# A new written-out order for a gated linear attention and a two-layer MLP on one core

## The chip, the cores and the metric

The kernel runs on one core of one Trainium2 chip. Time is device time in microseconds (us) of one execution; lower is better. Comparisons are made between executions on the same chip.

## What is computed

A gated linear attention with complex decays, for 4 batches, 8 heads, 768 tokens and 48 dimensions per head, and then a two-layer MLP over its output, 3072 tokens of 384 features with 2048 hidden ones:

```python
mag = np.sqrt(a_re * a_re + a_im * a_im)
scale = np.minimum(mag, 0.999) / (mag + 1e-06)
a_re_n, a_im_n = (a_re * scale, a_im * scale)
for t in range(S):
    ar, ai = (a_re_n[:, :, t, :, None], a_im_n[:, :, t, :, None])
    new_re = ar * S_re - ai * S_im
    new_im = ar * S_im + ai * S_re
    kv = np.einsum('bhd,bhe->bhde', k[:, :, t], v[:, :, t])
    S_re, S_im = (new_re + kv, new_im)
    y[:, :, t] = np.einsum('bhd,bhde->bhe', q[:, :, t], S_re)
...
h = x @ w_in
g = np.maximum(h, 0.0) + alpha * np.minimum(h, 0.0)
return (g @ w_out).astype(np.float32)
```

`x` is `y` with heads and dimensions merged. The two MLP weights come as 64-bit floats.

## The kernel before

The program is a set of tasks, each a Python generator that yields before every step (some instructions on one engine) and issues the step when it is resumed. The order of all steps is written out by hand as a text of 4292 letters, `ORDER`. Each letter stands for one task, and `Plan.run` (lines 96 to 98) resumes that task once per letter. What each engine gets, and in which order, follows from this text alone: every engine runs its own instructions in the order in which the letters issue them, and semaphores hold an instruction until its operands are there. A letter's place in relation to steps of other engines sets no time by itself.

```python
    def run(self, order):
        for c in order:
            next(self.tasks[self.LETTERS.index(c)], None)
...
        plan.run(ORDER)
```

The tasks, by letter (lines 950 to 963):

- A to I: nine gate stages (`gates`, line 223). A covers chunk 0 of batch 0 (128 tokens), B chunks 1 and 2, C chunks 3 to 5, and D to I three chunks each of batches 1 to 3. A stage loads `a_re` and `a_im`, works out magnitudes and running products of the decays on ACT, DVE and POOL, and stores decays (`decs`, line 323) and phases (`phs`, lines 421 and 431) to DRAM. L429 is its last DVE product.
- J, K, L: loads on SP's queue. J (`loads`) fetches for each unit queries and keys (`KQ`), phases (`PP`, L587) and decays (`T`, L594, in two halves). K copies values from DRAM to DRAM in the arrangement that a unit needs, L (`loads_v`) fetches values (`V`, `VL`).
- M, N, O: the pieces of the MLP weights and their conversion to 32 bits (ACT, POOL, DVE).
- P to m: 24 units (`unit`, line 645), one for each chunk of 128 tokens. A unit multiplies queries and keys by phases (L661, L663), then goes through six levels of doubling distance, from 1 to 32: a DVE product with the decays (L717), an ACT copy (L740 or L756), small score products on PE (L678), and masks (L702 on DVE, L699 on ACT). Then it transposes keys on PE (L785), ACT copies them to `T` (L787, L788), and PE makes the state products (L797) and the outputs (L817); DVE updates the state (L826, L829), PE adds its part (L841), ACT copies the result (L855) and two DMAs store it (`ysc`, L860).
- n: loads of the MLP input (`xT`, L873), for 14 groups of one chunk (the first and last two) or two chunks.
- o: the MLP (`all_mlp`, line 926). For each group and each of 16 feature blocks: three 128x128 products (L889, two passes each), ACT's relu (L896), DVE's leaky part (L898); then, for each chunk of the group, an output product (L908, two passes) that accumulates over the 16 blocks, and after the last block an ACT copy (L918) and a store.

The small products of the units use parts of the TensorE array (96x32, 64x64, 64x48, 96x48 weights), the transposes 96x128, the MLP's products 128x128. The buffers that bind are one `PP`, two `T`, one `V` and `VL`, three `KQ`, two tiles in PSUM for scores, two for features, one for an output row.

Of the kernel before, what the change touches and what calls it, by code (L numbers as in the profile page):

```python
# [27 lines left out]


ORDER = (  # L30
    "AAABAAAAAMAAAAAAAAAAAAAAAAAMMMBAAAAMJNAAAAAAAANJNNAAABANANAABBAABAJAKJABAAMAAAABBAAAAAABAOAAOAAKABAA"
# [4 lines left out]
    "MDLJLLCNCRMQDQCORQCQQORMCNKRCRoNODDCDOCNRQRCOQCOCCCCCQKOCMJQOLLoCRQLORCDCLLRKoDRQDLLLCCQNooooCQRRLCR"
    "QQDQCCoDJLLDoCCoCDCMoooRoDQoRCQLLLoRoDRRDCCCoooRoQDDCCRRDoNRRODRNRoooRRDooDnRRoRRoooooDOoLLJoRNOoJDo"
    "oooJDLooooRooLNooNoDRooOJRODROSSooRNoLooooooOooSooENooRSooRSoSJSNoRSERRLRSoSSooooOJLLSJLoooDoSooESJL"
    "LSoSSOoSSoJoLoooooEoLSLDSSDooooSoSSSTSJoSSDoooTSSSooDEToooDSESSSJDoSSooToooSooETJTSJLTLooTTDLoDDDDDE"
    "KSoooJToESSDoDTDoEToLoSKSoSDDoKSTTToooDoDoooJooDKEDSSoooDTTTDoLooTooLooooEooToEEJoEooUoTooUDEoooDooT"  # L40
    "DoDDoLTooJTLLLLLLTDooULooooTETTooTooDToEoDUDDDDDDDDTUoUooTTUoEooUnoUKDUDUKKoooToJJJDJEoETTTTLLLoUoDU"
    "DULEEoELoTUooTLKDoUDoELLoKDoTDDooDoDDDoooDEDTToEooLLoEooDoooUoooooTToTooDUooLDoEoTEoUooDooooUUEoooTo"
    "EoEoUoLUUooUUTEoUEEooULEoooUooUoEUKoJJEooEoooUEUJoJUUUUUoVUEUVJUUVFVVEooEUUUVooooooJoVJVEUUoEVFoEVEE"
    "JooVnVJoJooLVooooooFoWooooWVoVoFFVEEEELLLLLLVLLLooVVWooVooooooEVEEoEooWooWooVVVWoLLWWWEEEEEELEEVVVVV"
    "ooEoVooVLooFVWVEooVVJVJFJVJKVWEFVVWWWEoVJEEEEEVooWFLXLLLEEWEEooWooLoLooooLWEVVWEVEWEKWXEVVVVWLLLLWLo"
    "WFoooEWEEEELEoWoVVooWWEEooooLWEFFWooooooWoEJFoJoWooWWWJEEEEWoWWLoXLoLoEFFooooWoWooooJLLWXXXWFWWWoLXL"
    "ooLoXXWWLoJXWFooWoooXoJooFXoooFXXoXoXooXXJooXoLooFoooFoXXXXLoLYLXXoXLXJoonoXXoXoXooXJXoJJFGFYXFoXoYY"
    "FoFooGGoXXXFFXFKoKFKYFXYFFYFXFFooFFJYoLoooooLYoXoYXXXoJoFooLoFYFJFFGoLLLLoooooXoXXXYYoYoYYoYooYJJFoY"
    "oooooJooZoYYFFYYoZYGYoYoFoLFooooZoLoZooooJoFZZYLZYFoYoFFooJYFFFFFFFFFFFFFFFYoYLLLLoKGZGYYYYYJYZYKJoY"
    "YLLZYYGoLZGoooKoLoZYYKooLFFFGLZLLLGZYYFYZYZoFoFFFFFFFFoFKZZoZFFooFooaoFoFoooaooZGoZFLLLZLLFJZoFZFZJZ"  # L50
    "FZooZoFooZZGFFFoFFoonoooFooooGZoZooZaZFZoJZZoJooGoZZoJooZZaoooaaaGaZZZoZZJZLGJZZoaooLLLGoooooaGaoJoo"
    "oLbooKooJooooLGooabGaGbaoaGaoooGoaaoooooaoGoooLLGLooboobooboaabababaGaooaJoLLaaLoaoaooaaoGJLJGGGGoGo"
    "HGaaaHaaaoGJaaoabGGGGJbGLbGLaaLGHoLaaLooLaobcHGoaoooJJbooJoooGooHGbbooLGoHoobbobobcoooGGHbooGcoooooo"
    "oGGGGGGoHooooobbcbHbccbLLcGLLobHLbLooboGKGboGGGGobooobocbbLGcHcoocGoKbcGGJGGGGbbbHbbbKGbcbJGJccGGGcn"
    "LooJLLLGLGLLLcHLLLLLcHooLcoooGobbbcGcbbGGbbccooobGGooGooodoJJooocoHcGcHHGoocodooooooKGoooccJGGHoGooo"
    "oGooGcooococHGoJoHooGcccGdccoJcGcLGooodHHHLoHLooooJKoooLHddodHoHodododGodoooLLoooIcooodIoocdodHLdodc"
    "HcdLcoHdooccLLHLdIJoHHHcHooHoooocoLoodIdoddoKoodocddddoooeooddooLooodoHHooHooHKHoooLoodHoHodJdHHHHoH"
    "HHIJJdddddJedHoHndddHHdJJLdHeooJooLedodooeddeeoeoLooLHeeeIooHoooooHHHHHHHHHHooHKeoeJJeLoIIeooooofoLo"
    "LeLLLfeLLoooooeefIfooooooooeefeeeooefefoeeoHHHHHeeofIHoooHLLoeHfIooHHHooHeHeeeeIHeeeeeefJeHfoHJIoHeL"
    "oefHoJIoHLoJIffoffeJeIIeeLoofoJoooofHLLooofoogIoooffJfoofffoHofofofLooJLLLogofooJKLIofooHLoHogooongo"  # L60
    "HLLfoLgKHgHgooooooooooooofogogJIfgfffffIgIfffHLJIIoogfIIfILHKoHofHfooLLooooooggLgffgoooooogooooggoIo"
    "ooIHffgILIgogIgIogoLoILIoggooIgoJoLoooLoooILILIIoooogogooghIoLgohoggghhgJogJgggJggooKJgJJggIoIooghhJ"
    "gIIIIohoohgoooohoooooIIIIihIJIoIIIoIJoIooioIoohoJLhhJoooooooooLohLhIihIIIIIhiLoLLLLLLLLLLoonohoooooo"
    "hhoooohiohoihoohIIIIIoooihhhiohoJhJohiIhiioohooooIIIIIIIIIohoohhhhhhioooooooohhohooiohihhIIIooooiihh"
    "IiohhiooooooLoihohiJiiiLJLJLoLLLooooiLLLjLiooIIoiiJjooIojjIIioIIooooooooLojjjLIooooooiooioJoLoijoioo"
    "iiIijJiiijJLoIjiiiiiiiiiioIoooooooIiIoLoooInjLLoojjooooooLjjoooojoooJoojjoooJJooLjjjjjjjkkojooojoooo"
    "oooLkoLokLjoooojookkkkkoLLjooLLoLkookojokojjjjjkoJkkokLLokoooojjkJJJoooLooLoooookjookjkkjkokLjkoojoo"
    "kjojkoLokkooLoooooLooooLoooLoooojJolLLkjlLoookkoLokkkjkJkJkkkkkkoookooJlJoooooooookoLookolkJLklJJoko"
    "loooooloooonJooooJomoloolololoooooooooooooLoooooollllomolomloloooooloooooooooooLommlmLlLLooloooooooo"
    "ooooollolloommmmoLoloollooooooolmloLLLLLLoomlommmmllolllooolmommololmlmmlomlllloommLLLLLLmooLooooooo"  # L70
# [930 lines left out]
```

## Time and profile before

| | |
|---|---|
| runs shown | 836.15, 836.07, 830.36 us (median 836.07) |
| profiled execution | 831.98 us, of which the traced span is 830.2 us |
| mean granted TensorE clock | 0.991 |
| DMA | 58.4% of the 16 engines' span, 130.91 MB |
| L908 output products | 294.4 us of PE, 768 passes, mean 497 ns |
| L889 feature products | 296.3 us of PE, 1344 passes, mean 353 ns |
| L717 decay products | 146.8 us of DVE, 120 (of `KQ` with `T`), mean 1226 ns |
| L898 leaky part | 97.5 us of DVE, 224, mean 436 ns |

PE is TensorE's products, PEld its weight loads, DVE VectorE, ACT ScalarE, POOL GpSimd, SP the engine that issues DMAs. Products are pipelined, so a product's duration is longer than its distance to the next one, and the sum of durations of a group can exceed its busy time. "Idle before" and the waits name the engine and line whose result came last. The slices cut the span into 40 equal parts of 20.8 us; a digit is the busy share in tenths.

### The profile page before, as it was taken

The numbers are of one execution on the slowest core, as the hardware profiler recorded it, in microseconds if no ns is written. First come the engines' busy times: TensorE is split into PE (matmuls) and PEld (weight loads), VectorE is DVE, ScalarE is ACT, GpSimd is POOL, SyncE is SP. The second block draws the span as 40 slices with busy tenths as digits, with TensorE's granted clock in tenths as the row PEclk, the third lists the DMA queues.
The fourth block names the chain that finished last, engine by engine and source line by source line (L and its number), as shares of the span: only waits on it lengthen the run. The fifth ranks groups of instructions, "written<-read, shape, count | busy, mean of one in ns | idle before, by whom it ended". The sixth has DMA issues, their size and how long they took to land.

```text
span 830.2 us, 26838 instructions
## 1 busy us (share of the span) xinstructions
PE 692.1 (83%) x11488; PEld 525.0 (63%) x11488; DVE 650.5 (78%) x1020; ACT 441.5 (53%) x937; POOL 215.3 (26%) x293
## 2 busy tenths in 40 slices
PE   0001515789999999989999999999999999999998
PEld 0001414567777776767777777777777777777776
DVE  5999999999998899889998988999658644552112
ACT  7758879467636655564576456653443333333121
POOL 5231222617715601460155007310520000000000
PEclk9999997899999999999999999999999999999999
DMA  7597985785688489728874695458535544311110
GB/s 204 177 263 185 279 206 172 228 216 145 157 241 201 114 217 251 181 69 223 245 176 103 171 263 135 120 140 245 148 82 134 150 112 112 92 38 38 35 30 10
DMA packets 194174, 130.91 MB, mean 158 GB/s; under 512 B 74120, under 2 KB 185864, under 8 KB 194056
## 3 DMA queue, kind: packets, MB, share of 16 engines
q1 hardware_dynamic: 194056, 129.20, 58.4%
q8 instruction: 90, 1.47, 0.8%
q14 instruction: 28, 0.23, 0.1%
HBM read 100.82 MB, written 35.71 MB: 164 GB/s over the span
## 4 chain that ended last, share of the span: by engine, by line
PE 68%; DVE 14%; ACT 4%; POOL 4%; DMA 4%; issue 3%; SPq 2%; DVEq 0%; ACTq 0%; POOLq 0%
PE ps_o L908 27%; PE ps_h L889 26%; PE ps_lv L678 4%; PE ps_y L817 4%; DVE KQ L717 3%; PE ps_kv L797 3%; PE ps_y L841 2%; PE ps_kt L785 2%; DVE gate L338 2%; DMA T<-decs 1%; POOL gate L338 1%; POOL gate L340 1%; DVE gate L340 1%; DVE gate L298 1%; DVE gate L426 1%
## 5 line engine op out<-in xcount | busy, mean ns | idle before, releaser
L908 PE MATMUL ps_o<-w_out_sb,g_sb 128*128 128x384 f32 x768 | 294.4, 497 | 9.9 <-DVE g_sb L898 9.0
L889 PE MATMUL ps_h<-xT,w_in_sb 128*128 128x256 f32 (+1 forms) x1344 | 296.3, 353 | 1.2 <-issue 1.2
L889 PEld LDWEIGHTS ps_h<-xT,w_in_sb 128*128 128x128 f32 x1344 | 232.8, 191 | 71.3 <-issue 2.0
L896 ACT ACTIVATE g_sb<-ps_h 128x256 f32<-128x256 f32 (+1 forms) x224 | 79.0, 353 | 221.4 <-PE ps_h L889 220.5
L898 DVE SCALAR_TENSOR_TENSOR g_sb<-g_sb,al,ps_h 128x256 f32<-128x256 f32 (+1 forms) x224 | 97.5, 436 | 120.7 <-ACT g_sb L896 120.1
L908 PEld LDWEIGHTS ps_o<-w_out_sb,g_sb 128*128 128x128 f32 x768 | 136.1, 190 | 61.2 <-DVE g_sb L898 11.6
L717 DVE TENSOR_TENSOR KQ<-KQ,T 96x1024 f32<-96x1024 f32 x120 | 146.8, 1226 | 27.5 <-PE ps_lv L678 24.2
L678 PE MATMUL ps_lv<-WQ 96*32 96x32 f32 x2304 | 34.4, 204 | 77.5 <-DVE WQ L661 54.2
L678 PEld LDWEIGHTS ps_lv<-WQ 96*32 96x32 f32 x2304 | 26.4, 116 | 97.1 <-DVE WQ L661 54.2
L515 POOL TENSOR_SCALAR top<-top 128x768 f32<-128x768 f32 x16 | 44.8, 2802 | 82.3 <-ACT top L507 70.6
L740 ACT COPY WQ<-KQ 96x1024 f32<-96x1024 f32 x48 | 50.0, 1041 | 10.9 <-DVE KQ L717 10.8
L338 POOL TENSOR_TENSOR gate<-gate 128x72 f32<-128x72 f32 x42 | 25.9, 616 | 114.6 <-ACT gate L368 101.9
L338 DVE TENSOR_TENSOR gate<-gate 128x576 f32<-128x576 f32 (+5 forms) x84 | 48.0, 572 | 1.8 <-ACT gate L368 0.3
L756 ACT COPY W<-KQ 96x512 f32<-96x512 f32 x48 | 30.8, 641 | 31.2 <-DVE KQ L717 23.5
L699 ACT ACTIVATE A<-ps_lv,columns 128x64 f32<-128x64 f32 x144 | 38.1, 335 | 16.0 <-PE ps_lv L678 15.8
L817 PE MATMUL ps_y<-A,VL 64*48 64x64 f32 x2304 | 42.7, 224 | 3.9 <-issue 3.9
L855 ACT COPY T<-ps_y 48x256 f32<-48x256 f32 x96 | 31.4, 366 | 24.8 <-PE ps_y L841 23.9
L817 PEld LDWEIGHTS ps_y<-A,VL 64*48 64x48 f32 x2304 | 40.2, 126 | 5.6 <-issue 5.3
L426 DVE TENSOR_TENSOR gate<-gate 128x1152 f32<-128x1152 f32 (+2 forms) x36 | 43.1, 1219 | 0.4 <-POOL gate L411 0.3
L678 PE MATMUL ps_lv<-KQ,W 96*32 96x32 f32 x1536 | 24.9, 204 | 18.4 <-ACT W L756 18.2
L702 DVE TENSOR_TENSOR A<-ps_lv,mask 128x256 f32<-128x256 f32 x96 | 37.8, 413 | 0.0
L785 PE MATMUL ps_kt<-ident,KQ 96*128 96x96 f32 x192 | 25.7, 258 | 14.3 <-DVE KQ L717 9.3
(106 smaller groups left out, 916.1 us busy)
## 6 DMA issues: line engine op xcount, KB each, us to landing
T<-decs SPq DMA_DIRECT2D x48, 384.0 KB
PP<-phs SPq DMA_DIRECT2D x24, 387.0 KB
...
```

Source lines behind the costliest of these rows:

```text
L338: on(4 * k).tensor_tensor(out=m, in0=w[:, 1::-1].unsqueeze(2).to_broadcast([P, 2, 2, k]), in1=pairs_of(u), op=ALU.mult)
L426: TT(out=m[:, a], in0=U5[:, 1 + a], in1=turned(off3, o)[:, a].unsqueeze(1).unsqueeze(3).to_broadcast([P, L // 2, nb, 2]), op=ALU.mult)
L515: nc.gpsimd.tensor_scalar(out=top, in0=top, scalar1=F64_SMALL, scalar2=None, op0=ALU.max)
L678: nc.tensor.matmul(t[64 * i + j:64 * i + j + HC // 2, p], lhsT=keys(n, g), rhs=queries(n, g), start=True, stop=True)
L717: nc.vector.tensor_tensor(out=x, in0=x if x0 is None else x0, in1=m, op=ALU.mult)
L740: nc.scalar.copy(z.rearrange("p i n t -> p i (n t)").rearrange("p i (m h) -> p m i h", h=h), bass.AP(tensor=KQ.tensor, offset=KQ.offset + ...
L785: nc.tensor.transpose(t[:, p], KQ[:, 1, 4 * i + p], ident[:D2, :D2])
L817: nc.tensor.matmul(o, lhsT=Vp[h][64 * i:64 * i + 64, s, e_ * D:(e_ + 1) * D], rhs=a, start=False, stop=False)
L889: nc.tensor.matmul(p, lhsT=w_in_sb[:, f // 2, kk, f % 2 * P:(f % 2 + 1) * P], rhs=x_of[m][:, kk], start=(kk == 0), stop=(kk == NK - 1))
L896: nc.scalar.activation(gt, p, AF.Relu, scale=-1.0)
L898: nc.vector.scalar_tensor_tensor(out=gt, in0=gt, scalar=al_1[:, f:f + 1], in1=p, op0=ALU.mult, op1=ALU.add)
L908: nc.tensor.matmul(sums[0], lhsT=gt[:, c * P:(c + 1) * P], rhs=w_out_sb[:, f], start=(f == 0), stop=(f == NF - 1))
```

## The change

Only the text `ORDER` (lines 30 to 77) is replaced. The old and new texts have the same 4292 letters, each letter equally often, in another sequence; tasks, steps, instructions, tiles and buffers are the same. The new text comes from a planner that counts each change from small to large products dearer, and reads packet ends from the finished program; the planner itself is no part of the kernel. The first and last lines that differ:

```diff
 ORDER = (
-    "AAABAAAAAMAAAAAAAAAAAAAAAAAMMMBAAAAMJNAAAAAAAANJNNAAABANANAABBAABAJAKJABAAMAAAABBAAAAAABAOAAOAAKABAA"
-    "LMAAABAAABABBBLBALBABOAOMBAABLBBBNABAABABNAABABBNBABALABLOBOMBNBBKKONOBOBBNBBBJLBOBJBOBLBNBBBJBBBBBB"
-    "NBBNBBBKOBBPBPBPBBBBOPOLBNPBBCJBPCLOMBBCMNBKKBPKKKKBBPPBPMKCBPBBBOKOBCPBBBPPCBLBBJPPLPBNPKCCJCBCPCCC"
...
-    "oooooooooooooooooooooooooooommmmmmmmmmmmmmmoooooooooooooooooooonoooooooooooooooooooooooooooooooooooo"
+    "AAAAAAAAAABAAAAAAAAAAAAAAAMMMMAABAJJMAJJNAAANNLABANAAAABAAAABANAMBAAAABAMAAAANAAALAABKAAOBBAKAKAAAAA"
+    "KBBLLLBAAAALAOBABAAABKKBABOABABAABBMBBBAAKABABALABBBBOANBABABOANBNNBOOBKNOBKBONBNBLNOBBBBBMOBBBOBBJB"
+    "BBBBBKONBKJBPBBBPBBBBOBOOPPBKNJPBNBBCCMPOBBKBBPCCPBKKKMPCBBOBBNBPBPBPBCBBBCBLBPMKNJJPLBPLBBBPPBPPLLC"
...
+    "oLoooooooooooooooooooooooooomooooomommmmmmmmmmommmmmnooooooooooooooooooooooooooooooooooooooooooooooo"
     "oooooooooooooooooooooooooooooooooooooooooooooooooooooooooooooooooooooooooooooooooooooooooooo")
```

More of the change, by code (lines that the diff above doesn't have):

```diff
@@ L30 @@
 ORDER = (
-    "AAABAAAAAMAAAAAAAAAAAAAAAAAMMMBAAAAMJNAAAAAAAANJNNAAABANANAABBAABAJAKJABAAMAAAABBAAAAAABAOAAOAAKABAA"
-    "LMAAABAAABABBBLBALBABOAOMBAABLBBBNABAABABNAABABBNBABALABLOBOMBNBBKKONOBOBBNBBBJLBOBJBOBLBNBBBJBBBBBB"
-    "NBBNBBBKOBBPBPBPBBBBOPOLBNPBBCJBPCLOMBBCMNBKKBPKKKKBBPPBPMKCBPBBBOKOBCPBBBPPCBLBBJPPLPBNPKCCJCBCPCCC"
-    "JNNPCPCPBPCOLCPPPPPPPKNPCKPKNLJCPPJJPCDNPPKCPJCCCNDCPPOJKKCQPCNNPCPPOLJLNOCLCCMOMQCPQQCOQCQQCQCQCDPL"
-    "PDQPPPQCDDQQQCLQPNJCCOCQCOQCQCCQCNDCJLRCQQKQCCLnNJCRJLCDDDQQOCORNCCQNQQLOOQQCLKCOKCKRDCoDJNLDRNQCCNC"
@@ L36 @@
[L36 to L70, printed above, removed]
@@ L71 @@
-    "oomooolollooooooooooooooooooooooooooLooooooommmLLoLonooooooooooomLLmoooooooooooooooooooooooooooooooo"
-    "oooooooooooooooooooooooooooommmmmmmmmmmmmmmoooooooooooooooooooonoooooooooooooooooooooooooooooooooooo"
+    "AAAAAAAAAABAAAAAAAAAAAAAAAMMMMAABAJJMAJJNAAANNLABANAAAABAAAABANAMBAAAABAMAAAANAAALAABKAAOBBAKAKAAAAA"
+    "KBBLLLBAAAALAOBABAAABKKBABOABABAABBMBBBAAKABABALABBBBOANBABABOANBNNBOOBKNOBKBONBNBLNOBBBBBMOBBBOBBJB"
+    "BBBBBKONBKJBPBBBPBBBBOBOOPPBKNJPBNBBCCMPOBBKBBPCCPBKKKMPCBBOBBNBPBPBPBCBBBCBLBPMKNJJPLBPLBBBPPBPPLLC"
@@ new lines @@
+    "CNJBONLOCPNKPCJPPJCNPCPCPOPNPPPCDDJPPCPPCOPCCPCPCPNJPPMCCCCPCPLNJCPCMQPCQCCNQQKKQCDOLCOQCQCPQJPDPPCQ"
+    "QODCPQMCDQQPCKQQCPQNDJCNDCDQCNCDQCLCJJLLJJJNKCDKKNCRCNROCQLLCCJOOQMRnCROCQNLDRQQMCLOQCQJDRRCLQDRCLLO"
+    "NCKRCLCCooLQDRCNCOQROQCQCODQDoQQCQQCQRDCONKCNQCCCOCQNMCROCCODCCQCMOQLLDKCLoLRoLDCoRCoCooDRLooLDLLQoo"
+    "RDoJoCLRDooDoQLNCRRRCCCDCCCDLRLCoDoLDCRRCCooQQCoRoRRQQQQRRRoRNDoRRRRoRoRNoDCooQooLoDooooRoLLDoOoLDoL"
+    "oOoLRDooNRODJJJoRoooDLoLoSSRRooNLoRNoRoELRoRSRooOooooNooOoSoJoJNSSoooSNESoSoOSJRSoSoOOoooooSoSLELSSO"
@@ new lines @@
+    "ooSoSoSoLoooooJSnDSoESoJSDSSJTLJJoSSSDoooooSoSooSKDoTooSSSDSoSTDooEJDDTSDDSoKEoTSooooTEoSoTLTLSoSETK"
+    "oToSoTETSooEDooooDoSTToTSoJLooooLJJoESETooLoooooTToToDDDDDDDDDDoooDEUDoTLLooToEooEoLoooUoSooLSoKoJTJ"
+    "LoEoToooooooTTUTToooTToooTDoEoULLoDDDDLDDLDoDJTJnJToDoDDDEDDDEoUUoTKKKKUoDDoooDoTUTooooEoUTJTUoTKDDD"
+    "UEUUEDDLEUTETEToLETDDUETDEDLoDoLoooDooDoooooToDDoooUTooLLEoDooooLLooEDUooDooooUoDooUooTTEooEoToUUoUo"
+    "UUoUoooEEoULEUUTEUooLooLLoUoooEooUEoELoooUUEUUUoUUoUUUJoEVVVJoUoUVJEVEJJUoEUFoFVoEUoEUoooVVoJJVVoLVV"
@@ new lines @@
+    "oVJLoooLonJoJEVoLoWoooEWEEELFoVFLVVoooooooooVLVWVVEoLELoEoooLooWoFoEoooWEEWEVVVVWVEVoEELLEEoVEoEEEEE"
+    "EEVEFEJoVVVoooLWWLoJWJoEVoJVoVJWVooEWVVEVVWLLLLLVELEELFLVEWWLXWFWWoooEoWooEEVoLoFLFFoEEFEVVVEVEVVWWW"
+    "WoWWVoooooEWWEVoEEWoLoooLWWooEoWXWoLJoooooooJooFWWJWoWEEWoLWLJoooWoWoEFoFJoXooFXWoEoWWXXWXLXoooWooWL"
+    "XWFoLWXLXooooEooooFoLWoLXXXJLXJFXXXFoXoJooFFLooooooooXLLLXoXooXXXXXoYoJXoXLXooXYooXXXXYooXooGGnoFFFJ"
+    "ooXFFFFFFFXXYFXYLGFLYXXXLoXLYFooYooXooXFXFYXooYYJooJJFFFooooXooooYoJLYYYYYoooLLLYFLYFooJFooFFFoooFYZ"
@@ new lines @@
+    "oZoYoYJLoGooYFoYoLYJGoYYoFFooZoJYooFFFFYZoJooLYoLoGoLZoZoKKYGKooYoFoYYJKFYKJYYFZFLFLZFFFGLZZYYYFFFFF"
+    "FFYYGYoYYFYYoFFZGoooLoFoooaFGoZFFFLooZFZZFoFZZFooZYZoooLoLLFoFFooLFaGooKZKGFZoZZZYZLLLLLZFooJFJFFoZo"
+    "FFFoZZFoZoooooooFGZoooZoFoaaZZZFZZZGFooGZJJoJZonooooooaaZZZZZoaZaaZLaLoLoLaooGooooaFoZJZoJoGoooooGoo"
+    "ooJoaoGoaaoooJaobGoaGoobbabLHLoooGaLoLobLHoGooLLGGoGooobLoLaHbKaaaaboobaooJoaJGaaoJboaJooGaHKoGoaobo"
+    "aaGaaaJboKGGGaKabaGGoaaGGGaaaaGaacKGKooGoooboooHGooLoGoobHcGGbGGGGGooooGGoooooboHHJbbboooJLLLcocLLLo"
@@ new lines @@
+    "GLboGoooGGoooLLoccbbccbGHoGoobbbHoHHbbbGoooGGbGGGGGGGGGGGGooLooJLnooLKGLcbbcoboooooHJcoccJoHHocobbbb"
+    "bGobcocGbKccJJcoGoGLGLobcbocGbdGLLLLLLGLLGHbobbHoobbHGoooooooooooccccLLdoGcGbocHcbcGoLGcLooGoGoGGJoc"
+    "JcoooooooooooGooHKGGGGcccHHdcccLJoHHodoLooLJHooooJJoHcocooddddLHoodooooododHooooHHHHHLdcododoooododI"
+    "JooooooddodoooooLLccocccdoLdLLHeHdHHHHoLocoIooLcoIddcdedododdodooooooLLooodKJoHHHHooooodnoJodddIdddd"
+    "doLdJdddddddoodoeJHoeHJoJJoooHHHHeHHeeLeooeooeJeoIoooooooooJeIeoeeeLHHoooeeoHoofoeoIfoIooLJKHLoofoee"
@@ new lines @@
+    "oHIeoHoooeIeefeofLeLLofLLeeILoHofffoHHLHIHoHLeeoHHeoLooeeJeeeKeeIeeJeJIfeoeeHHIHHHHHHHHHHHJHLLLLHLLo"
+    "ILeHHgoooooofoeHoeooeJoIIJfJooofoofffIofooHHfooooIogoHHLHHLfoILoHooogoIoooooogoffgggffJoggfooKfofJHg"
+    "ffLooooooofofggoofnoLLIofILKoHoooHofffffHKgIggfoggoooooIHoogLLLLLLLoHoogoofoIHoooooooooooIgfIgHIgggK"
+    "gIgILfLLLHIIfffLoffoLofffIooJoJgoIJIIgIogoooooIogoggIooIIIIIIIoooooooooogggIIggggIgggJJoJJhJLhLhJgog"
+    "oohooogooohooooooogghiooohohoooohhJoihhKIIIIIIIooooooLhooLLoLLLLohhhhhhooohoLoILooooooooJLoooohIioio"
@@ new lines @@
+    "hILIhJiJJJhhhJiIoooLiIioIhhoonhhhooohhoIIIohhhhhhohhhhohhhohhhohoiohIoLiIIIIIiIiLooIILLoLoJoooiioLoi"
+    "oiioJjiIioIIooooLoLoojojIoJoojoooILLoooiIiiijjjijooLioIoiLIoiLoiIioooIoIooIIIILoIIoIoooIIIiJooiooioo"
+    "oooooooiiiioiiijjijLiijiiJiiiioiooooojjoooooJJJJoooooooooojoooooojjkkoooooooooooookjooooLkoooojkjjjk"
+    "okjLLjoLjjLjLLLjLoJnLoLjooojojLooLooooojoooookojkkjkjjkjkkokkJJJoooooojkkoookjoooooojoLLLLojkkjjjjoL"
+    "ooLokkkooooooLLoLkokkkoLkokojjLLoLoLJoookoojookooookkkjkkkkkoJkJkklokkkLkkoooJLoooooooooololloooooJl"
@@ L73 @@
+    "lJlkJJlLLLlLlJolooooLLoooooooooooooolooooooomooonmlLlololLolJolLlmoooooooooooooooooooooooomooomlmlol"
+    "lloolmmllloomlooooooLolooomooLomloLoloooooooooooollllmlmmmmLmlLLooooooooomolooloooooomooommllllollom"
+    "lomoooooooooooooooomllnmmomooooooooooooooooooooooooomoooomoooooLoomooooLLooLoLLLLLoooooooooooooooooo"
+    "oLoooooooooooooooooooooooooomooooomommmmmmmmmmommmmmnooooooooooooooooooooooooooooooooooooooooooooooo"
     "oooooooooooooooooooooooooooooooooooooooooooooooooooooooooooooooooooooooooooooooooooooooooooo")
```

## The prediction

> **What bounds the kernel now.** I read the page's busy shares and slices first, then busy time by stretches, then the TensorE timeline and the waits.
>
> ```profile
> span 830.2 us, 26838 instructions
> PE 692.1 (83%) x11488; PEld 525.0 (63%) x11488; DVE 650.5 (78%) x1020; ACT 441.5 (53%) x937; POOL 215.3 (26%) x293
> PE   0001515789999999989999999999999999999998
> DVE  5999999999998899889998988999658644552112
> PEclk9999997899999999999999999999999999999999
> ```
>
> DVE is full from the second slice on, PE only from the tenth. So there are two stages. The stretches put numbers to them (columns: window, its length, busy time and count on PE, PEld, DVE, ACT, POOL, granted clock, DMA share, GB/s):
>
> ```profile
> 40.00:80.00 40.00, 3.94 (x192) 3.13 (x192) 37.95 (x72) 26.09 (x35) 9.40 (x6) 1.00 0.81 220
> 120.00:160.00 40.00, 24.18 (x574) 19.61 (x575) 38.99 (x71) 28.03 (x52) 17.39 (x8) 0.83 0.71 217
> 200.00:230.00 30.00, 28.27 (x504) 21.98 (x503) 28.65 (x42) 18.95 (x43) 22.03 (x27) 1.00 0.59 152
> 450.00:500.00 50.00, 50.00 (x749) 37.75 (x748) 45.44 (x65) 25.25 (x57) 5.58 (x13) 1.00 0.77 209
> 790.00:830.00 40.00, 36.66 (x218) 27.25 (x212) 7.98 (x23) 8.64 (x29) 0.00 (x0) 1.00 0.07 20
> ```
>
> Up to 230 us DVE sets the pace: from 40 to 230 it is busy 184.5 of 190 us, so only 5.5 us are idle; in the first 40 us 10.1 are. From 230 on PE sets it: 586.7 busy of 600.2 us. The 13.5 us left are 3.5 after the last product (it ends at 826.75), 6.8 of "issue", in which PE waited for nothing the profile shows, and 3.1 of waits for another engine, the only ones an order can take away:
>
> ```profile
> PE ps_kv L797 <- ACT T L788: 1.5, 1, 1.5
> PE ps_kt L785 <- DVE KQ L717: 1.2, 1, 1.2
> PE ps_kt L785 <- ACT T L788: 0.4, 1, 0.4
> ```
>
> What a change between small and large products costs is read from the TensorE timeline (start, us, engine, line, names, shape, count):
>
> ```profile
> 486.27 1.45 PE L908 MATMUL ps_o<-w_out_sb,g_sb 128*128 128x384 f32 x4
> 487.56 0.50 PE L785 MATMUL ps_kt<-ident,KQ 96*128 96x96 f32 x4
> 487.89 1.49 PE L889 MATMUL ps_h<-xT,w_in_sb 128*128 128x256 f32 x6
> 489.21 0.50 PE L785 MATMUL ps_kt<-ident,KQ 96*128 96x96 f32 x4
> 493.45 1.46 PE L889 MATMUL ps_h<-xT,w_in_sb 128*128 128x256 f32 x6
> 494.84 1.15 PE L797 MATMUL ps_kv<-V,T 64*64 64x48 f32 x64
> 498.40 1.56 PE L908 MATMUL ps_o<-w_out_sb,g_sb 128*128 128x384 f32 x4
> 499.79 1.46 PE L889 MATMUL ps_h<-xT,w_in_sb 128*128 128x256 f32 x6
> ```
>
> Four output passes take 1.29 us from start to start (486.27 to 487.56); right after small products they take 1.39 (498.40 to 499.79). Six feature passes take 1.29 elsewhere and 1.39 before small ones (493.45 to 494.84). So a change costs about 0.10 us each way. The transposes (L785) are cheaper: 1.29 before them, 1.32 after (487.89 to 489.21), 0.03 in all.
>
> **The change part by part.** Every letter occurs as often in the new text as in the old (4292 letters), so the same instructions run on the same engines; none is added or removed. Reading the letters against each task's steps gives every engine's queue before and after; sums of row durations along these queues show what moved.
>
> *The frame stays.* At the last step of each unit the DVE work queued up to there differs by -6 to +10 us, PE work by -9 to +7. At the first feature product of each group DVE differs by -4 to +6 us, PE by at most 3. So at 230 us PE should have done what it has done now.
>
> *Changes on PE.* Runs of large products are entered 131 times before and 125 after. Without the transposes the edges fall from 88 + 88 to 81 + 80. Of them 133 before and 126 after lie behind the first feature product of group 2 (222 us), where PE sets the end: 7 x 0.10 = **-0.7 us**. The other 8 lie under DVE, which hides them; without that cover they are worth another 0.8. [...]
>
> *Waits of PE for other engines after 230.* Before the state products (L797) less than 1 us of PE work lies behind ACT's copy in 19 of 24 units now, in 13 then. I scale the 1.9 us of the two ACT rows by 13/19: **-0.6**. All three rows gone would be -3.1. On the other side, output products with under 1.5 us of PE work behind their DVE step go from 23 to 25 of 384; before 230 such a wait was 9.0 us in 6 cases, 1.5 each, so two more are +3.0. I take the lower value, because after 230 that wait has no row at all.
>
> *DVE in the first stage.* Between 40 and 245 us of DVE work I count 151 steps that need another engine's result; under 0.6 us of DVE work lies in between in 65 now and 66 then. I take **0**. Ends: -3.8 (the named DVE waits there, 2.3 of them for ACT) and +5.5 (the idle time doubles).
>
> *Gates.* The gate stages of units 9 and 12 (letters E and F) end behind 9 and 10 us more DVE work than before, so the phase store, its reload into `PP` on SP's queue and the unit behind it come closer: DVE work from the stage's last product to the unit's first step goes from 20.6 to 14.9 and from 15.2 to 14.1. The stage of unit 3 ran with 14.5 now (155.8 to 168.2 us) and its unit did not wait, so **0**; without cover the unit would wait for the store, 3.1 us in the chain.
>
> *Loads on SP's queue.* Of a unit's decay loads (`T`), the second is placed with under 1.3 us of DVE work ahead of its first use (L717) in one unit now (unit 5, 0.3) and in eight then (units 0, 5, 6, 9, 10, 13, 19, 23). Such loads were in the chain:
>
> ```profile
> 44.21 6.68 DMA T<-decs
> 183.14 5.67 DMA T<-decs
> ```
>
> Yet unit 5's load went out at 205.9 and its use began at 211.3 without a wait; DVE waited for T 0.7 us in the whole run. SP runs ahead of where the text places it, so I take **0** and make the other end a rival. For unit 13 an output row's store (which waits for ACT) now stands before both T loads; before, it stood behind.
>
> Sum: -0.7 - 0.6 = -1.3 on the profiled execution's 831.98 us, which gives 830.7. That execution lies 4.1 below the median of the runs shown (836.07; two at 836.1, one at 830.36), so the same program spreads by 0.7%. From the median the sum gives 834.8. I take the middle, **832.5**.
>
> **The rivals.**
>
> *Late decay loads (slower).* If SP does not run ahead in the seven new places, DVE waits about 5.7 - 0.7 = 5 us in each. Units 0 and 6 lie where DVE paces (57 and 251 us): 10 us. Units 9, 10 and 13 cost 15, against 15.4 us that DVE has idle from 300 to 450 (4.7 + 4.9 + 5.8), so they hide behind PE's work in hand; units 19 and 23 come where DVE is under 70% busy. 832.5 + 10 to 14 is 842 to 847. It decides from the point where SP issues the second load less than 5.7 us ahead of its use. For: eight places instead of one. Against: unit 5.
>
> *The clock drops in the PE stage (slower).* After PE gaps of 4.5 and 3.1 us (before 121 and 125), the granted clock was 0.84, 0.65 and 0.83 in the three 10 us windows from 130 on: 6.8 us of clock lost. A gap of that size after 230 would cost itself and these, 4.5 + 6.8 = 11: 844. Against: the longest gap there is 1.65 us now. [...]
>
> *Everything tightens (faster).* The wins at their outer ends: 1.5 for all changes, 3.1 of PE waits, 3.8 of DVE waits, 8.4 in all: 823.6. For: more cover before the small products. Against: 65 and 66 tight places on DVE.
>
> *The text does not do what it says.* Changes dearer should mean far fewer of them; 131 to 125 is little. This is in the forecast already.
>
> **How the numbers follow.** Forecast 0.52, late loads 0.15, clock 0.08, tight 0.25. Within 1% of the median (827.7 to 844.4) is about what a measurement of this kernel can tell from no change. I put the tight case below that band and both slow cases above: faster 0.25, same 0.52, slower 0.23. The range reaches from 823, the tight case, to 845, inside the late-load case; the forecast's own ends are 823.6 and 839.2 (830.7 + 3.0 + 5.5).
>
> **What would show it.** Right: PE starts its unbroken work at 225 to 235 us, DVE idles 4 to 8 us from 40 to 230, and named PE waits after 230 stay under 4 us. A row "DVE KQ L717 <- DMA T<-decs" of several us shows the first rival; a PEclk digit under 9 after the tenth slice the second. I would be wrong if PE fills earlier or later by over 8 us, or if the pitch of 1.29 itself changes.

## The result, and the profile after

The new order is slower by about half a per cent: 838.92 us (median of 20 runs, 833.74 to 844.17) against 835.69 us (20 runs, 830.36 to 842.62). The ratio is 1.0046 [1.0023, 1.0068], some 3.8 us; a second comparison, later, gave 1.0067 [1.0037, 1.0096]. The brackets hold 95% intervals. The ratios leave out executions that lie over 1.5% above the fastest of their kernel, as the profiled one of old_then_new_again does. The forecast was 832.5 us.

The page of the profile after (its execution took 837.28 us), with the lines that answer to those shown of before:

```profile
span 835.6 us, 26825 instructions
PE 697.2 (83%) x11488; PEld 528.2 (63%) x11488; DVE 651.8 (78%) x1020; ACT 439.7 (53%) x937; POOL 223.6 (27%) x293
PE   0002416979899999999999999999999999999998
DVE  5999999989899899988999978989668553634112
PEclk9999657789999999999999999999999999999999
```

The work is the same, and so are the two stages. The lower clock digits of slices five to nine are not the order's: the page of a second profile of before (before_again, below) has the digits 8, 5, 6 and 8 in slices five to eight, and of the 20 executions after, the 9 with a mean clock over 0.98 took 838.4 us on average, the others 839.0. What differs lies around the seam, the place at about 240 us where DVE stops setting the pace and PE begins to. The stretches of after (window, its length, busy time and count on PE, PEld, DVE, ACT, POOL, granted clock, DMA share, GB/s):

```profile
160.00:200.00 40.00, 33.94 (x608) 25.79 (x606) 35.63 (x60) 25.77 (x49) 11.62 (x12) 0.91 0.80 204
200.00:230.00 30.00, 25.49 (x554) 20.12 (x553) 26.56 (x39) 18.40 (x44) 25.86 (x32) 1.00 0.52 125
450.00:500.00 50.00, 49.55 (x690) 36.94 (x693) 44.87 (x62) 24.46 (x58) 6.07 (x9) 1.00 0.69 185
```

DVE, which sets the pace there, is busy 26.56 of the 30 us from 200 on, where it was busy 28.65. From 40 to 230 us it idles 10.8 us in place of 5.5. The waits name where (DVE until 245 us: engine, line, for whom, us in all, times, longest):

```profile
DVE g_sb L898 <- ACT g_sb L896: 6.3, 6, 2.5
DVE WQ L661 <- issue: 2.4, 1, 2.4
DVE KQ L717 <- DMA T<-decs: 0.7, 1, 0.7
```

The first row was 2.3 us in 3 waits before (longest 1.3); the second and the third are new (before, the one wait of DVE for `T` was unit 19's, in the second stage). In the timeline of DVE after, the long ones stand at the head of these two rows (start, us, engine, line, operation, names, shapes, count, and in brackets the idle time before it):

```profile
168.93 1.22 DVE L661 TENSOR_TENSOR WQ<-KQ,PP 96x1024 f32<-96x1024 f32 x1 [2.41 <-issue]
...
210.17 0.35 DVE L898 SCALAR_TENSOR_TENSOR g_sb<-g_sb,al,ps_h 128x128 f32<-128x128 f32 x1 [2.47 <-ACT g_sb L896]
```

The first is unit 3's first product. It needs the phases `PP`, which SP reloads from the gate stage's store. The timeline of SP's queue shows what the reload stands behind:

```profile
161.72 2.85 SPq L626 DMA_DIRECT2D VL<-in_v_dram  x3
164.62 0.59 SPq L587 DMA_DIRECT2D PP<-phs  x1
```

It is issued at 164.62. In before it was issued at 162.53, and unit 3 began at 168.19 without a wait:

```profile
162.53 0.32 SPq L587 DMA_DIRECT2D PP<-phs  x1
```

The second wait is for a relu, and ACT's timeline shows why that relu is late:

```profile
204.95 0.27 ACT L896 ACTIVATE g_sb<-ps_h 128x128 f32<-128x128 f32 x1
208.58 0.22 ACT L366 COPY runs<-gate 128x36 f32<-128x36 f32 x1 [3.36 <-POOL gate L340]
...
209.78 0.20 ACT L368 ACTIVATE runs<-gate 128x18 f32<-128x18 f32 x1
209.88 0.26 ACT L896 ACTIVATE g_sb<-ps_h 128x128 f32<-128x128 f32 x1
```

Two gate copies (letters D, lines 366 and 368) stand ahead of that relu, the first of them waits for POOL, and ACT stands still for 3.36 us with relu work behind it. The place is not new. In before ACT stood at the same copy, and DVE then waited for the relu behind it:

```profile
202.48 0.22 ACT L366 COPY runs<-gate 128x36 f32<-128x36 f32 x1 [2.73 <-POOL gate L340]
...
202.91 0.35 DVE L898 SCALAR_TENSOR_TENSOR g_sb<-g_sb,al,ps_h 128x128 f32<-128x128 f32 x1 [1.32 <-ACT g_sb L896]
```

So the new order adds 1.15 us here and 2.41 at unit 3. What else the first row gained (2.8 us) lies in shorter waits, which change places from profile to profile.

To find when the loss arises I count work, not time: each product with its usual distance to the next one (0.32 us for an output pass, 0.22 for a feature pass of two chunks, 0.015 for a small product). PE had done its first 90 us of products at 237.2 us before and at 243.2 us after. So the first stage ends 6.0 us later, more than the whole loss in the spans (5.4). Behind that point, what remains of the time once PE's waits, its "issue", the lower clock and the end after the last product are taken off is 579.7 us before and 580.6 after. The waits of PE for others after 230 us did not fall:

```profile
PE ps_lv L678 <- ACT W L756: 2.5, 5, 1.1
PE ps_lv L678 <- issue: 2.0, 2, 1.4
PE ps_o L908 <- DVE g_sb L898: 1.1, 2, 0.6
PE ps_h L889 <- issue: 1.1, 2, 0.6
PE ps_kt L785 <- DVE KQ L717: 1.0, 2, 0.6
PE ps_y L817 <- issue: 0.9, 2, 0.6
PE ps_h L889 <- DVE g_sb L898: 0.2, 1, 0.2
```

Without "issue" they are 4.8 us, against 3.1 before. The 1.5 us of L797 are gone (the forecast had scaled them down), but waits for ACT's `W` stand in their place.

### The profile page after: what moved, and what is told of

The parts are those of the page before. It is cut to its first block, busy times and chain, and to the rows that moved or that the text cites. A ratio compares the mean times of both kernels' runs of the same rounds, so it can differ in the third digit from the quotient of the medians.

```text
span 835.6 us, 26825 instructions
## 1 busy us (share of the span) xinstructions
PE 697.2 (83%) x11488; PEld 528.2 (63%) x11488; DVE 651.8 (78%) x1020; ACT 439.7 (53%) x937; POOL 223.6 (27%) x293
## 3 DMA queue, kind: packets, MB, share of 16 engines
q8 instruction: 90, 1.47, 0.7%
## 4 chain that ended last, share of the span: by engine, by line
PE 48%; DVE 25%; POOL 9%; DMA 5%; ACT 5%; issue 4%; SPq 3%; DVEq 0%; POOLq 0%; ACTq 0%
PE ps_o L908 20%; PE ps_h L889 18%; DVE KQ L717 5%; DVE gate L338 4%; PE ps_lv L678 3%; POOL gate L338 3%; DVE gate L340 3%; PE ps_y L817 2%; POOL run L340 2%; DMA T<-decs 2%; PE ps_kv L797 2%; PE ps_y L841 1%; DVE g_sb L898 1%; SPq L626 1%; DVE gate L426 1%
## 5 line engine op out<-in xcount | busy, mean ns | idle before, releaser
L889 PE MATMUL ps_h<-xT,w_in_sb 128*128 128x256 f32 (+1 forms) x1344 | 300.0, 356 | 5.3 <-DMA xT<-ysc 4.0
L717 DVE TENSOR_TENSOR KQ<-KQ,T 96x1024 f32<-96x1024 f32 x120 | 149.9, 1253 | 22.5 <-PE ps_lv L678 15.3
L338 POOL TENSOR_TENSOR gate<-gate 128x72 f32<-128x72 f32 x42 | 28.0, 666 | 138.2 <-ACT gate L368 135.5
L515 POOL TENSOR_SCALAR top<-top 128x768 f32<-128x768 f32 x16 | 49.3, 3083 | 57.1 <-ACT top L507 51.6
L855 ACT COPY T<-ps_y 48x256 f32<-48x256 f32 x96 | 31.4, 364 | 32.4 <-PE ps_y L841 31.5
L817 PE MATMUL ps_y<-A,VL 64*48 64x64 f32 x2304 | 42.2, 224 | 5.3 <-issue 5.3
L817 PEld LDWEIGHTS ps_y<-A,VL 64*48 64x48 f32 x2304 | 40.0, 126 | 7.1 <-issue 7.1
L318 POOL TENSOR_TENSOR gate<-gate 128x72 f32<-128x72 f32 (+2 forms) x18 | 18.7, 1041 | 69.8 <-DVE gate L318 68.9
```

The costliest lines, as they stand in the source:

```text
L338: on(4 * k).tensor_tensor(out=m, in0=w[:, 1::-1].unsqueeze(2).to_broadcast([P, 2, 2, k]), in1=pairs_of(u), op=ALU.mult)
L515: nc.gpsimd.tensor_scalar(out=top, in0=top, scalar1=F64_SMALL, scalar2=None, op0=ALU.max)
L717: nc.vector.tensor_tensor(out=x, in0=x if x0 is None else x0, in1=m, op=ALU.mult)
L817: nc.tensor.matmul(o, lhsT=Vp[h][64 * i:64 * i + 64, s, e_ * D:(e_ + 1) * D], rhs=a, start=False, stop=False)
L889: nc.tensor.matmul(p, lhsT=w_in_sb[:, f // 2, kk, f % 2 * P:(f % 2 + 1) * P], rhs=x_of[m][:, kk], start=(kk == 0), stop=(kk == NK - 1))
```

## The experiments

My theory after the result: the loss is all in the first stage, in the two waits above. The rival: the later order loses too, by waits that a single profile shows only in part.

**Half old, half new.** Since every letter only resumes its task, any beginning of one text can be followed by what is left of the other, in the other's sequence.

```diff
-ORDER = new
+ORDER = old[:1232] + rest of new     # old_then_new_245, cut at about 245 us
+ORDER = old[:841] + rest of new      # old_then_new_187, cut at about 187 us
+ORDER = new[:1231] + rest of old     # new_then_old_245
```

> The old order up to about 245 us (its first 1232 letters), the new order for all that is left. Theory: the new order loses its time in the first stage alone (DVE idle 10.8 instead of 5.5 us from 40 to 230 us; PE is 6.0 us late at the same amount of work by 243 us and gets 0.6 back later). Then DVE idle from 40 to 230 is 5 to 6 us, PE enters its full stage as early as before, and the ratio to before is 0.998 to 1.000. Rival (the loss lies in the later order, the early one is the chance of one execution): the ratio is 1.003 to 1.007.

> The old order up to about 187 us (its first 841 letters), then the new order. Theory: of the 6 us that DVE falls behind by 245 us, 2.9 arise before 190 us of DVE work (unit 3's wait for its phases) and 3.6 behind it (DVE waiting in its queue for the MLP's leaky steps). So here only the second part is left: DVE idle from 187 to 245 us about 4 us more than before, ratio 1.002 to 1.004. Rival (all of it comes from unit 3's late load): ratio 0.998 to 1.000 and no wait of DVE over 1.5 us behind 187 us.

> The new order up to about 245 us (its first 1231 letters), the old order for all that is left. Theory: the whole loss stays, and what the new order gets back later is missing: DVE idle from 40 to 230 near 10.8 us, PE 6 us late at 245 us, ratio 1.005 to 1.008. Rival (the loss lies in the later order): ratio 0.998 to 1.001.

> The kernel before, profiled once more: what one execution's profile is worth. If the 5.5 us of DVE idle time from 40 to 230 us belong to the order, they come again within 1.5 us; if they are chance, they move by 3 us or more.

Measured: old_then_new_245 1.0030 [0.9997, 1.0063], old_then_new_187 1.0070 [1.0032, 1.0108], new_then_old_245 1.0028 [1.0001, 1.0054]. The cut at 187 us lies within the early part and loses more than the whole order, so that seam costs by itself and tells little. The repeated profile of before took 831.56 us, with 6.3 us of DVE idle from 40 to 230 us, so that figure does belong to the order. Both halves were then repeated.

> The new order up to 245 us, then the old one, timed once more (first 1.0028, 1.0001 to 1.0054), for the early part alone. Theory (the early order costs DVE 4 to 6 us of waits before 245 us, and nothing hides them): ratio 1.003 to 1.006, PE has done 90 us of work by 241 to 244 us (old order: 237.2 and 238.3). Rival (early waits are chance or hidden): under 1.002.

> The old order up to 245 us, then the new one, timed once more (first 1.003, 0.9997 to 1.0063), for the later part alone. Theory (the later order has some 1.7 us more of PE waits on ACT and DVE, by five profiles of it and three of the old one, and drops of the granted clock behind them): ratio 1.001 to 1.004; PE waits for other engines after 245 us 4.5 to 6 us. Rival (the later order costs nothing): under 1.001, waits near 3.7.

> The new order as it is, on the same chip as the others (1.0046 before). If early and later part add up, its ratio is the sum of the two above, 1.004 to 1.008; DVE idle from 40 to 245 us 10 to 12 us again, PE at 90 us of work by 241 to 244 us.

They gave 1.0024 [0.9994, 1.0055], 1.0024 [0.9996, 1.0053] and 1.0067. Each half costs about a quarter of a per cent, and together they make the whole: my first theory held only half of the loss. Three of the four intervals reach to no change; the two runs of a half taken together do not (by my estimate 0.26% ± 0.20 early and 0.27% ± 0.22 later). In new_then_old_245 the DVE rows of the first stage are the same again:

```profile
DVE g_sb L898 <- ACT g_sb L896: 4.3, 4, 2.5
DVE WQ L661 <- issue: 3.3, 1, 3.3
```

PE's first 90 us of work end at 241.0 to 243.2 us in five profiles with the new early order (three texts, all with unit 3's wait) and at 237.2 to 239.6 in eight with the old one: 242.2 against 238.5 on average, 3.7 us. DVE's idle time from 40 to 230 us agrees: 10.4 us on average in these five, 6.5 in the eight.

The second stage has to be read over several profiles too. In the four with the old order there (before, before_again, new_then_old_245 and its repetition) and behind 240 us, PE's waits for other engines are 3.7 us on average, its "issue" 5.8, and the time lost to a lower clock 0. In the ten with the new order from 245 us or earlier they are 5.3, 5.5 and 2.4. So the later half has 1.7 us more of named waits and 2.4 more of lost clock, and no more of "issue".

**The two early waits, mended.** Moved letters in the new text:

```diff
-OoLDoLoOoLRDooNRODJJJoR   # loads_first: J25 to J27 (PP, T of unit 3)
+OoJJJLDoLoOoLRDooNRODoR   #   ahead of the value load L45
-ooDEUDoTLLooT             # copy_later: gate copies D60, D61
+ooEUoTLLoDDoT             #   behind the relu o148
```

> The new order with one edit on SP's queue: unit 3's phases and decays (PP, two halves of T) are issued ahead of three value loads that stood before them. Theory: DVE's wait before unit 3's first product (L661, 2.41 and 3.34 us in two executions) falls under 0.7 us, the T wait behind it (0.67, 0.78) goes too, and DVE idle from 40 to 230 us falls from 10.8 to 7.5 to 8.5. Rival (DVE waits there for something else than this load): the wait stays over 2 us.

> The new order with one edit on ACT's queue: two small copies of gate stage D (L366, L368), which wait for POOL's product, go behind the relu of an MLP block instead of ahead of it. Theory: DVE's wait for that relu near 210 us (L898, 2.47, 2.14 and 2.47 us in three executions) falls under 0.5, and PE's idle 1.9 us before the output product there goes; DVE idle from 40 to 230 falls from 10.8 to 8 to 9. Rival (POOL is late anyway and DVE waits elsewhere for it): the 2.5 us turn up as another DVE wait before 230 us.

> Both edits together, the rest as in the new order. Theory: DVE idle from 40 to 230 us is 5 to 6.5 us as before the change, PE is no more than 2 us behind the old order at 245 us, and the ratio to before is 0.998 to 1.002 (the new order: 1.0046). Rival (these waits are hidden by PE's work in hand, and the loss comes from the later order): ratio 1.003 to 1.006.

One execution each of the first two: 836.15 and 844.22 us. Both edits together, timed: 1.0028 [0.9994, 1.0062]. Unit 3's wait fell to 1.4 us in loads_first, not to nothing: from the end of the gate stage's last product (L429) to unit 3's first, the chain of store and reload takes 11.6 us there, and the new order leaves only 10.2 us of DVE work beside it (11.7 before). The copy only handed its wait on: POOL is late whatever stands behind it, and in copy_later DVE's row is

```profile
DVE g_sb L898 <- ACT g_sb L896: 4.0, 3, 2.6
```

with the 2.6 us now at the next relu. So this wait for a late engine was not moved away by a few letters. Nor do these edits prove that the two waits carry the early loss: in both_early PE's first 90 us of work end at 240.3 us with 8.3 us of DVE idle, but in both_early_and_late, whose text is the same up to unit 11's loads, at 244.7 with 11.0. That they do is read from the rows of the five profiles.

**The later waits, mended.** Three loads that came late in profile after profile were moved forward, first with the early edits, then behind the old beginning:

```diff
-YZLLLLLZFooJFJFF   # J82, J83 (T of unit 11) ahead of L148
+YZJJLLLLLZFooFFF
-JoJJhJLhLhJg       # the state step h2 of unit 18
+JoJhhhLLJJJg       #   ahead of four loads
...                 # J138, J139 ahead of o936
```

> Both early edits and three later ones on SP's queue: the decays of unit 11 ahead of five value loads, the state row of unit 18 (St) ahead of two key and two value loads, the decays of unit 19 ahead of an output row's store. Theory: the repeated waits go (L717 of unit 11 for T 1.7 to 1.8 us, L725 of unit 18 for St 3.2 to 4.1, L717 of unit 19 1.3) and with them PE's idle 1.4 and 1.1 us before L678 near 389 and 607 us; ratio 0.994 to 0.999, under that of the two early edits by 0.002 to 0.003. Rival (PE's work in hand hides them): the same ratio as the two early edits within 0.001.

> The old order up to 245 us, then the new one with three edits on SP's queue: unit 11's decays ahead of five value loads, unit 18's state row ahead of two key and two value loads, unit 19's decays ahead of an output row's store. Theory: DVE's wait for unit 11's decays (1.7 to 3.4 us in five executions of this part) goes, and with it the PE wait and the clock drop near 390 us; ratio 0.001 to 0.004 under that of the same order without the edits, so 0.998 to 1.001. Rival (PE's work in hand hides these waits): the same ratio within 0.001.

Measured: 1.0039 [1.0008, 1.0070] and 1.0028 [0.9998, 1.0058]. In the second, PE's gaps between 450 and 700 us fell to 0.9 us (3.9 in old_then_new_245), and the time was that of the unmended half. These waits had been covered; the loss of the later order was elsewhere. What the mended profile still showed was this (PE's timeline, unit 6):

```profile
276.14 0.75 PE L817 MATMUL ps_y<-A,VL 64*48 64x64 f32 x40
281.00 1.83 PE L817 MATMUL ps_y<-A,VL 64*48 64x64 f32 x56 [4.11 <-issue]
```

PE stops for 4.11 us in the middle of 96 alike products, waiting for nothing that the profile names. Such stalls stood at products 3132, 4146, 5539, 5919 or 9723 in profile after profile, whole multiples of 126.7 products apart, in either order. The page counts 90 packets and 1.47 MB on the queue "instruction", each of 16,384 bytes; PE's 11,488 products and as many weight loads over 90 packets are 255 instructions a packet. So the suspicion: PE stalls at the ends of packets of its own program. The trace's records of these packets bear it out. Behind 240 us the 20 profiles hold 121 unnamed PE stalls over 0.25 us, and 119 of them end 1.20 to 1.69 us after such a packet has landed; of the 110 waits of that size for a named engine or DMA, 7 do. The packet of the stall above landed at 279.69 us, and PE went on at 281.00. No two of these packets began less than 3.30 us apart.

**Moving the packets.** 64 transposes that nobody reads are put ahead of everything, while PE is idle (in before_shifted they start at 1.64 us and take 8.42, and the first product of the work starts at 54.34), and shift all later packet ends by half a packet:

```diff
     plan.add(all_mlp())
+    early = ps.tile([P, HP, D2], F32, tag="misc", name="ps_kt")
+    for _ in range(64):
+        nc.tensor.transpose(early[:, 0], ident[:D2], ident[:D2, :D2])
     plan.run(ORDER)
```

> The old order, with 64 transposes of the identity matrix put ahead of everything on PE, into a PSUM tile that nobody reads (some 6 to 10 us while PE is still idle, before its first product at 54 us): nothing of the work moves but the count of PE's instructions, by half of the 126.7 products at which its unexplained stalls recurred. Packet theory: the stalls without a releaser lie again at 126.7k+89 counted with the added products, so 64 products earlier in the work; in the middle of unit 11's V products (product 5919 of the work, 1.00 and 1.26 us in the two profiles of the old order) and of unit 18's (9723, 1.63 and 1.08 us) there is none above 0.25 us. Rival, that the stalls belong to a place in the work (its buffers, its operands): they stay where they were. Time: 0.998 to 1.003 of the kernel before by either.

> The kernel old_then_new_mended (1.0028 of the kernel before) with the same 64 transposes ahead of everything. Its largest single loss was a stall of 4.11 us at product 3132, inside unit 6's V products at 281 us, with a granted clock of 0.83 behind it. Packet theory: no packet ends there any more, the stall goes, and if it carries the loss of the later order the time comes to 0.998 to 1.001. Rival, that the loss is the order's own waits and the clock that falls behind them: the stall goes or stays and the time stays at 1.002 to 1.004.

Measured: 1.0321 [1.0275, 1.0367] and 1.0395 [1.0348, 1.0443]. The expected times were far off, and the places were right. Counted with the added products, the stalls lie on the same grid of 126.7 (5033, 5539, 6047, 6935 and so on), so 64 products earlier in the work, and the one at 3132 in unit 6 is gone. But there are many more of them. PE's waits behind 240 us in before_shifted:

```profile
PE ps_y L817 <- issue: 9.8, 9, 2.1
PE ps_y L841 <- issue: 7.4, 5, 3.2
PE ps_h L889 <- issue: 4.7, 2, 2.7
PE ps_lv L678 <- issue: 4.3, 3, 2.0
PE ps_kv L797 <- ACT T L788: 1.5, 1, 1.5
PE ps_kt L785 <- DVE KQ L717: 1.2, 1, 1.2
```

The named waits are those of before; "issue" went from 6.8 to 26.2 us and the clock loss behind the seam from 0 to 8.5. With 1.9 us at the seam and 1.7 in the rest that is the whole 31.5 us between the two spans. Where they come is seen in PE's timeline there, in one of the units:

```profile
512.55 1.15 PE L797 MATMUL ps_kv<-V,T 64*64 64x48 f32 x64
513.52 0.29 PE L808 MATMUL ps_y<-ident,nothing 64*48 64x256 bf16 x4
513.63 1.52 PE L817 MATMUL ps_y<-A,VL 64*48 64x64 f32 x96
515.08 0.54 PE L841 MATMUL ps_y<-KQ,St 96*48 96x64 f32 x11
517.64 0.77 PE L841 MATMUL ps_y<-KQ,St 96*48 96x64 f32 x21 [2.03 <-issue]
```

One packet ends among the state products at 513 us, the next some 2 us later, because the small products here take 0.015 us each: a packet of them alone is gone before the one behind it is there (that one landed at 516.21 us). I counted, in 19 profiles (all but that of old_then_new_again), the packets behind 240 us by the time that PE took for them, its waits left out, and those with an unnamed stall over 0.25 us at their end. A packet's end is set at every 126.7 products from the 89th on:

```
time for the packet   packets   stalled   mean stall   longest
under 3 us               42        30       1.02 us      3.22
3 to 5                  223        43       0.22         3.21
5 to 7                  380        41       0.13         4.25
7 and more              685         1       0.00         0.53
```

Profiles with the old order from 245 to 300 us have no packet under 3 us in the second stage, those with the new order there one, the two shifted kernels 16 each.

**Unit 6, and where the later loss arises.** The old order was kept as far as behind that place, and unit 13's loads, which the prediction had flagged, were moved alone and together with it:

```diff
-ORDER = old[:1232] + rest of new       # old_then_new_mended, late loads moved
+ORDER = old[:1551] + rest of new       # old_to_300_mended, the same loads moved
-ooLoGoobHcGGbGGGGGooooGGoooooboHHJbbboooJLL   # mended_unit13, old_to_300_unit13:
+ooJJLoGoobHcGGbGGGGGooooGGoooooboHHbbboooLL   #   J96, J97 (T of unit 13) ahead of L166
```

> The old order up to its letter 1551 (about 300 us, behind unit 6's V products), the new order from there, with the late loads of old_then_new_mended moved as there. If what is left of the later order's loss (1.0024 to 1.003) arises between 245 and 300 us, where PE stalled inside unit 6 and unit 7's decays then came late: 0.998 to 1.001, and the stall at product 3130 is under 0.5 us as in the two profiles of the old order. If it arises behind 300 us: 1.002 to 1.004 again.

> old_then_new_mended with unit 13's two T loads (J96, J97) put ahead of the output store L166 and task o588 that the new order places in front of them. Late-load theory: unit 13's wait at its first decays product (3.1 us in that profile) and PE's wait of 2.13 us behind it go, and the time falls by 1 to 2 us, to 1.000 to 1.002. Rival (PE has work in hand there, or the wait passes on to the next unit): the wait goes or shrinks and the time stays at 1.002 to 1.004.

> old_to_300_mended once more, for its place against the kernel before (0.9962, 0.9929 to 0.9994). If the stretch from 245 to 300 us carries all of the later part's loss, as read from packet 24 of PE's instructions (in the ten profiles with the new order there, packets 23 and 24 went by in 1.7 to 1.9 and 5.0 us and PE stalled 2.4 us behind them on average; in the five with the old order there, in 2.8 and 4.5 us, with 0.35 us): 0.995 to 1.000, and no stall over 1.5 us at product 3130. If 0.9962 was chance and the loss lies behind 300 us: 1.002 or more.

> old_to_300_mended with unit 13's T loads (J96, J97) ahead of L166 and o588 as in mended_unit13, where the time went from 1.0028 to 1.0006 with overlapping intervals. If that move is worth its 1 to 2 us here too: 0.994 to 0.997 and no wait of unit 13's first decays product over 1 us; if the wait was covered: 0.995 to 1.000 as old_to_300_again, within each other's intervals.

Measured: 0.9962 [0.9929, 0.9994], 1.0006 [0.9975, 1.0038], 0.9979 [0.9956, 1.0002] and 0.9986 [0.9960, 1.0011]. With the new order from 245 us: 1.003, 1.0024, 1.0028, 1.0006. With the new order from 300 us only: 0.9962, 0.9979, 0.9986. So the runs put the later loss between 245 and 300 us; behind 300 us the new order, with its late loads moved, loses nothing and may be a little faster. Single intervals of the two groups overlap in part; all three of the second group lie below all four of the first. Like with like, the late loads moved in both, the averages are 1.0017 of two and 0.9976 of three, by my estimate 0.41% ± 0.27 apart.

What differs in that stretch is seen in PE's timeline, some 8 us ahead of unit 6's stall. In before:

```profile
265.52 0.46 PE L678 MATMUL ps_lv<-WQ 96*32 96x32 f32 x32
265.91 1.56 PE L908 MATMUL ps_o<-w_out_sb,g_sb 128*128 128x384 f32 x4
267.40 0.46 PE L678 MATMUL ps_lv<-WQ 96*32 96x32 f32 x32
267.67 0.49 PE L678 MATMUL ps_lv<-KQ 96*32 96x32 f32 x32
268.01 0.46 PE L678 MATMUL ps_lv<-KQ,W 96*32 96x32 f32 x32
```

And in old_then_new_mended, where the last row goes on with more of the same:

```profile
267.65 0.81 PE L908 MATMUL ps_o<-w_out_sb,g_sb 128*128 128x384 f32 x2
268.39 0.46 PE L678 MATMUL ps_lv<-WQ 96*32 96x32 f32 x32
268.67 0.47 PE L678 MATMUL ps_lv<-KQ,W 96*32 96x32 f32 x31
268.94 0.21 PE L678 MATMUL ps_lv<-WQ 96*32 96x32 f32 x2
```

The new order has taken the four output products from between 32 and 96 score products: one change less. The packet that held these now takes 2.5 to 2.7 us instead of 3.5 (1.7 to 1.9 and 2.8 in the expectation above, which set its ends elsewhere), and at the end of the next one, inside unit 6's output products (L817), PE stalls 2.0 us on average in ten profiles (0 to 4.25) against 0.5 us in seven with the old order there (0 to 1.74). That the short packet itself never had the stall, but always the one behind it, I can't explain. The packet that PE then lacked began to be fetched 0.6 to 7.4 us after PE had entered the one before it in the ten profiles, 0 to 5.1 us in the seven; what sets this delay no run here shows. My expectation of no stall over 1.5 us with the old order fell short by a little: old_to_300_again has 1.74. Its PE timeline:

```profile
277.68 0.79 PE L817 MATMUL ps_y<-A,VL 64*48 64x64 f32 x40
280.21 1.12 PE L817 MATMUL ps_y<-A,VL 64*48 64x64 f32 x56 [1.74 <-issue]
...
282.09 2.93 PE L908 MATMUL ps_o<-w_out_sb,g_sb 128*128 128x384 f32 x4
```

It also shows what can follow such a stall: four output passes take 2.93 us, where 1.45 is usual, because the granted clock is 0.5 for 3.41 us from 281.69 on. In the 19 profiles it fell so 25 times behind 240 us, for 3.41 or 6.83 us. In 24 of these cases a PE gap of 1.43 to 4.25 us had begun within the 5 us before, 21 times an unnamed stall and three times a wait for ACT. Not every such gap has this effect: one of 2.70 us passed without.

The stall's mean difference, 1.5 us, is not the whole of the later loss (0.24 to 0.30%, 2.0 to 2.5 us). From PE's product 2600 to 3600 (some 250 to 306 us) its gaps and the clock lost come to 4.4 us on average in the ten profiles and to 3.2 in the seven, because the old order stalls at other packet ends there, up to 2.63 us at product 3259. A second difference lies there too: PE waits for DVE's leaky step at product 2852 in all ten (0.3 to 1.7 us), in one of the seven (0.55). So the timed runs point to the place, and the profiles account for part of the loss there. No run took away the stall and nothing else.

Unit 13's loads: DVE's wait of 3.1 us there fell to 0.5 us in mended_unit13 and to 1.5 us in old_to_300_unit13 (from 2.1). With the beginning to 300 us the time did not follow; with the other one the intervals overlap.

## Why the prediction was wrong, step by step

A gain of 1.3 us was forecast and a loss of some 3.8 us came. The two gains did not show, and the first stage, whose DVE waits were taken at nothing, made about half of the loss. That 838.92 us lies between 823 and 845 is luck: the upper end stood for late decay loads, which did not decide. Two of the prediction's own signs had failed in the profile of after: DVE idled 10.8 us (4 to 8 were named), and PE's named waits after 230 were 4.8 us (under 4).

- **The frame stays: wrong.** PE's first 90 us of work ended at 243.2 us in place of 237.2, 3.7 us later on average over profiles; equal sums of queued work at the marks say nothing of waits between them.
- **DVE in the first stage, 0: the step that failed first.** The idle time rose by 5.3 us (3.9 on average over profiles), which is nearly its outer end of +5.5. I had counted places with little DVE work ahead of a foreign result, 65 and 66, and took equal counts for equal waits. By the wait rows two places made most of it, and what they lacked was not DVE work in general but work beside one chain: the store and reload of unit 3's phases (2.4 to 3.5 us in five profiles, none before), and a relu queued behind a gate copy that waited for POOL (2.5 to 2.6, before 0.6 to 1.3). In the timed halves the early part is worth 0.24 to 0.28%; that these two waits are its cause is read from the rows, and no edit took them away.
- **Gates, and "SP runs ahead", 0: wrong for unit 3.** I had named its cover of 14.5 us as the proof that units 9 and 12 were safe, and had not asked what became of unit 3 itself. The figure was too high as well: from 155.8 to 168.2 us are only 12.4, and DVE was busy in 11.7 of them. In after 10.3 are left, and the reload went out 2 us later behind three value loads. Units 9 and 12 did not wait, as forecast. For unit 13, where I had flagged a load behind a store, the wait came (1.0 us in after, 3.1 in old_then_new_mended), and the time did not need it: 0 was right there.
- **"Issue", no term: a step left out.** The prediction set the 6.8 us of "issue" aside, since PE then waited for nothing the profile shows, and called 3.1 us the only waits that an order can take away. Nearly all such stalls end just after one of the packets has landed (119 of 121 over 0.25 us behind 240 us), an order moves them, and the description of the change says that the planner reads packet ends. In sum they did not grow with the new order (5.8 and 5.5 us on average), but 64 products more at the start made them 26.2.
- **Changes on PE, -0.7: not found, and with the other sign at one place.** Behind the seam the rest without waits is 579.7 and 580.3 us in two profiles of before, 580.6 and 579.6 in two of after. That spread hides a gain of 0.7. At unit 6 a change that was saved, worth 0.2 us by my rows, made a packet of small products shorter and was followed by stalls of 2 us on average.
- **PE's waits after 230, -0.6: half right.** The wait at L797 went, as the sum had it; others took its place, +1.7 in all in that profile and on average over profiles (5.3 against 3.7). Behind 300 us the order, with its late loads moved, was 0.14 to 0.38% below the kernel before. That is near the 1.3 us (0.16%) of both terms together, but only one of three intervals excludes no change.
- **The rivals.** Late decay loads: units 0 and 6 did not wait, and unit 3's 0.7 us is the only wait for `T` in the first stage, so no. Behind 245 us DVE waited 5.0 us for `T` in after (0.7 before), and moving these loads did not change the time. The clock: in the profile shown of after it cost nothing behind the seam, but it drops there in eight of the nine other profiles (old_then_new_again left out) with the new order from 245 us or earlier, 2.4 us on average over the ten. So this rival came in part, and the prediction had given it 0.08. The 6.8 us of clock that it priced by the gaps before 121 and 125 began at 136.8 us, nearer to gaps of 2.42 us (before 134.62) and 3.81 (before 142.73). Behind 240 us, 24 of 25 drops followed gaps of 1.43 us and more, not only such as the 3.1 and 4.5 I had named; 21 of these gaps were unnamed stalls, three waits for ACT. A drop followed a gap of 1.43 us, and none followed one of 2.70. Nothing tightened: both the DVE waits of the first stage and the PE waits of the second rose.
- **The starting point.** I took the middle between the low profiled execution and the median. The kernel before has medians of 834.2 to 836.6 us in all comparisons, so the sum should have stood on the median: 834.8 in place of 832.5.
